# Second attention of a three-stage kernel: packed rows as the stationary operand, block-wise turns on VectorE, and two softmax steps on GpSimd

## The chip, the cores and the metric

One Trainium2 chip, one NeuronCore of it. The metric is the device time of one execution in microseconds (us). The kernel is one launch; its inputs and its output lie in the chip's memory (HBM). The engines are named as the profile names them: PE is TensorE (its matmuls) and PEld its weight loads, DVE is VectorE, ACT is ScalarE, POOL is GpSimd, and SP is SyncE, which starts most of the transfers.

## What is computed

Three layers follow each other: an attention in two steps, a mixture of eight experts of which every token takes two, and a feed-forward layer with SiLU. The change lies in the second step of the attention.

```python
def sm_attn(qq, kk, vv):
    s = scale * np.matmul(qq, kk.transpose(0, 1, 3, 2))      # scale = 1 / 8
    s = s - np.max(s, axis=-1, keepdims=True)
    a = np.exp(s)
    a = a / (np.sum(a, axis=-1, keepdims=True) + 1e-09)
    return np.matmul(a, vv)
p_packed = sm_attn(p, k, v)          # p [4, 8, 32, 64], k and v [4, 8, 576, 64]
out = sm_attn(q, p_packed, p_packed) # q [4, 8, 576, 64]: 32 keys for each of 576 tokens
...
x = out as [2304 tokens, 512]
logits = x @ w_gate; noise_scale = np.log1p(np.exp(x @ w_noise))
top2 of logits + noise_scale * noise; two experts relu(x @ w1[e]) @ w2[e], weighted
...
h = x @ w_in; out = (h / (1 + exp(-h))) @ w_out
```

## The kernel before

**Tiles and units.** The 2304 tokens are 18 tiles of 128. A tile is made of the tokens of one batch, or (two of the 18, `r == 8`) of the last 64 tokens of two batches. The first attention runs in eight units `packed(b, g)` of one batch and four heads, the second in ten units `unpacked(t, n, lg)`: eight of two tiles (`n` = 2) and two of one tile. Every unit is a generator with four steps, and the loop over `slot` (0 to 15) issues the steps of several units per slot, by the lists START1, START2, LAG1 and LAG2. After slot 9 the steps of `route(0, 11)`, the routing of the first 11 tiles, come in between; from slot 12 on (SWITCH) other PSUM pools are in use. The order on each engine is then set by the framework's planner, which works with its own costs; every engine runs its own queue strictly in order.

**`unpacked`, the function that is changed.** Step 1 turns q on PE (`qp`, L380) and copies it to `qT` (ACT). Step 2 makes the scores: a matmul with `qT` stationary (128 columns) and `ppT` moving (64 columns) per head, L387, or L394 for the one-tile units; the profile calls their output `s`. The scores lie in PSUM as tokens by (head, 32 keys). DVE takes the maximum (L397), subtracts it (L399), ACT takes the exponential (L400), DVE sums (L401), adds 1e-9 (L402), inverts (L403) and multiplies (L404). Step 3 turns the 128 x 128 pieces back on PE (`a2p`, L409) and copies them to `a2T` (ACT, L50 in the profile, the helper `cp`). Step 4 multiplies by `ppBD` (`xp`, L418, 272 columns: 256 of x and 16 logits), adds the two logit halves on DVE (L422, L420), copies x to `xr` (ACT) and writes `xr` to `xs` in HBM (SP, L425). `xr` has two buffers.

**What lies around it.** `packed` makes scores with 32 packed rows stationary at four column positions of the array and 256 columns of k moving (`s`, L320; 64 columns in L323), and in the same way `pp` (L346, 64 columns). POOL copies four pieces of `pp` to `ppBD` (L354) and makes the low halves of the first expert's weights (L111, 128 x 1024, eight times, `wa0l` to `wa7l`). The tiles `wa0h` to `wa7l` hold k and v first: `wa6l`, for one, is v of `packed(3, 0)`, so the split of `wa6l` must come after the `pp` matmuls of that unit. At the end `route(0, 11)` gives `idx0` (DVE, L502); POOL gathers rows with it (L154), PE turns them (`tps`, L144), and the first expert's matmuls (`hps`, L166 to L168; `acc`, L176 to L178) begin, with `route(11, 7)` beside them. What follows (experts 1 to 7 and the SiLU layer) is one dense run of matmuls.

Of the kernel before, what the change touches and what calls it, by code (L numbers as in the profile page):

```python
# [7 lines left out]
F32 = mybir.dt.float32  # L8
# [6 lines left out]
OP = mybir.AluOpType  # L15
AX = mybir.AxisListType
# [3 lines left out]
P = 128  # L20
# [4 lines left out]
CAP = ET * P  # L25
# [18 lines left out]
def body(ctx: ExitStack, tc: tile.TileContext, q, k, v, p, wg, wn, noise, w1, w2, w_in, w_out, out):  # L44
# [70 lines left out]
    def tick():  # L115
        """Finish the loads that were started DELAY ticks ago."""
        later.append(None)
        while later.count(None) > M["delay"]:
            fn = later.pop(0)
            if fn:  # L120
                fn()

    def load(dst, src, c, eng=V):
        """src [c * 128, 1024 / c] -> dst"""
# [14 lines left out]

    def transposed(src, xh, xl, j):  # L140
        """src [128 rows, 512] -> columns j*128.. of the split xh, xl [128, 4, n]"""
# [7 lines left out]
    def fetch(src, ix, c0, n):  # L149
        """The rows of src that the columns c0..c0+n-1 of ix name"""  # L150
# [8 lines left out]
    def first(ws, x, f, n):  # L159
        """[128 f, n] of w1.T x"""  # L160
# [55 lines left out]
    with ExitStack() as ax:  # L216
# [13 lines left out]
        # k, v and q wait in the tiles that the first expert and its rows will need  # L230
# [44 lines left out]
        # p turned, once above and once below zeros; group 0's second copy is the ninth  # L275
# [24 lines left out]
        def packed(b, g):  # L300
            """The packed rows of four heads, pp = softmax(p k^T / 8) v, in four steps."""
# [65 lines left out]
        def unpacked(t, n, lg):  # L367
            """x and the logits lg [128, n, 16] of tiles t..t+n-1, in four steps."""
# [14 lines left out]
            s2 = pS2[0].tile([P, n, 8, 32], F32, name="s2", tag="s2")  # L383
            if r < 8:
                b = parts[0][0]
                for h in range(8):
                    T.matmul(s2[:, :, h, :], qT[:, h, :], ppT[b, h // 4][:, h % 4], start=True, stop=True)  # L387
            else:
                for h in range(4):
                    for b, sl in parts:  # L390
                        o = 128 * (h % 2)
                        m = ppT[b, h // 2].rearrange("p j o k -> p (j o k)")
                        m = m[:, o:o + 128].rearrange("p (a k) -> p a k", a=4)[:, 0:4:3, :]
                        T.matmul(s2[sl, 0, 2 * h:2 * h + 2, :], qT[:, h, sl], m, start=True, stop=True)  # L394
            s2f = s2.rearrange("p n h k -> p (n h) k")
            mx = sb.tile([P, 3, 8 * n], F32, name=f"mx2{n}")
            V.tensor_reduce(mx[:, 0, :], s2f, axis=AX.X, op=OP.max)  # L397
            sd = sb.tile([P, 8 * n, 32], F32, name=f"sd{n}", tag="sd")
            V.tensor_tensor(sd, s2f, mx[:, 0, :, None].to_broadcast([P, 8 * n, 32]), op=OP.subtract)  # L399
# [4 lines left out]
            V.tensor_tensor(sd, sd, mx[:, 2, :, None].to_broadcast([P, 8 * n, 32]), op=OP.mult)  # L404
            yield
            anf = sd.rearrange("p a b -> p (a b)")
            ap = pTr.tile([P, 2 * n, P], F32, name="a2p", tag="tr")
            for i in range(2 * n):
                T.transpose(ap[:, i, :], anf[:, i * P:(i + 1) * P], ident)  # L409
            aT = sb.tile([P, 2 * n, P], F32, name=f"a2T{n}", tag="a2T", bufs=4)  # L410
            cp(A, aT, ap)
            yield
            for i in range(n):
                xr = sb.tile([P, 2, 256], F32, name="xr")
                for g in range(2):
                    xp = pMx.tile([P, 272], F32, name="xp", tag="m")
                    for b, sl in parts:
                        T.matmul(xp[sl], aT[:, 2 * i + g, sl], ppBD[b, g], start=True, stop=True)  # L418
                    if g:
                        V.tensor_tensor(lg[:, i, :], xp[:, 256:272], lg[:, i, :], op=OP.add)  # L420
                    else:
                        V.tensor_copy(lg[:, i, :], xp[:, 256:272])  # L422
                    cp(A, xr[:, g, :], xp[:, 0:256])
                r0 = (t + i) * P
                nc.sync.dma_start(xs[r0:r0 + P, :], xr.rearrange("p a b -> p (a b)"))  # L425
            yield

        def route(t0, n, lg):
            """Two experts, their gates and slots for the tiles t0..t0+n-1."""
# [3 lines left out]
            # log(1 + exp(z)) = log 2 + z / 2 + log(cosh(z / 2)); by its series where |z| <= 1/2  # L433
# [32 lines left out]
            # slot - 63.5 = CAP * expert + the number of earlier rows of the expert - 63.5  # L466
# [50 lines left out]
            # row of ys: the first TA tiles of all experts come before the others  # L517
# [48 lines left out]
        for slot in range(START2[-1] + LAG2[-1] + 1):  # L566
            if slot == SWITCH:
# [60 lines left out]
    def load64(raws, sbuf, src, last=None):  # L628
        """Loads src [128, a, b], float64 as words, 512 a row; the function returned makes its float32 value."""
# [15 lines left out]
    def routed():  # L645
        ctx = mx = ExitStack()
        with mx:
# [13 lines left out]
            def convert():  # L661
                """One [128, 512] piece of the float64 weights to its float32 values in DRAM"""
# [14 lines left out]
            def combine(m):  # L677
                t0, n = BLOCKS[m]
                xh, xl = X["ab"[m % 2]]
                # rows of the first TA tiles have earlier rows too few to fill more than TA tiles of an expert  # L680
# [220 lines left out]
```

## Time and profile before

| | |
|---|---|
| time, median of 3 runs | 1022.69 us (1022.52 to 1023.4) |
| the profiled execution, first to last instruction | 1020.1 us (its own device time is not given apart from this span) |
| PE busy | 987.6 us (97%), 6056 matmuls |
| DVE, ACT, POOL busy | 448.4 us (44%), 357.0 us (35%), 211.2 us (21%) |
| chain of work that ended last | PE 91%, DMA 3%, DVE 2%, ACT 1%, issue 1% |

The span is one execution under the profiler. A row of a group of instructions gives the line, engine and operation, output <- inputs, the form, the count, then the busy time and the mean of one, and last the idle time before them with what ended it. In the chain of waits each row is a start, a length and the work that ran; a chain follows back from the last instruction to whatever released each step. Matmuls overlap, so the pitch of a row of matmuls is read from the chain, where each piece counts once.

### The profile page before, as it was taken

To read this page: it belongs to the slowest core of one execution; us is meant where nothing else is said; L and a number is where in the kernel's file an instruction comes from. 1 tells how busy PE (TensorE), PEld (TensorE's weight loads), DVE (VectorE), ACT (ScalarE), POOL (GpSimd) and SP (SyncE) were. 2 spreads that over 40 slices of the span, in tenths; PEclk is the share of its full clock that TensorE was granted. 3 is DMA by queue.
4 is the path that set the end of the run, shared out by engine and by line. 5 is a ranking of instruction groups with operands and counts; after the bars stand their busy time and mean duration, and the time that the engine had idled before them with its cause. 6 is when DMAs were issued, how large, how long until landed. Compare 5 with 4: busy or idle time off the path is not lost.

```text
span 1020.1 us, 15287 instructions
## 1 busy us (share of the span) xinstructions
PE 987.6 (97%) x6056; PEld 876.7 (86%) x6056; DVE 448.4 (44%) x877; ACT 357.0 (35%) x693; POOL 211.2 (21%) x253
## 2 busy tenths in 40 slices
PE   6988798999999999999999998999999999999997
PEld 4766678899999989999998988999999999998996
DVE  3557762565656565665634447222232231112111
ACT  3566322443434343343423354222222222223332
POOL 2152011110101010010100117343232332222222
PEclk9998699999999999999999999999999999999999
DMA  9992224574756566574723445111110111000000
GB/s 247 246 274 88 73 73 157 189 234 148 228 179 221 186 206 204 184 236 152 234 86 101 137 154 166 52 31 32 36 39 19 52 31 31 1 1 32 1 21 21
DMA packets 80477, 122.53 MB, mean 120 GB/s; under 512 B 14608, under 2 KB 47376, under 8 KB 80400
## 3 DMA queue, kind: packets, MB, share of 16 engines
q1 hardware_dynamic: 74320, 101.57, 31.9%
q0 software_dynamic: 6080, 19.93, 6.5%
q8 instruction: 49, 0.80, 0.3%
q14 instruction: 28, 0.23, 0.1%
HBM read 93.17 MB, written 28.31 MB: 119 GB/s over the span
## 4 chain that ended last, share of the span: by engine, by line
PE 91%; DMA 3%; DVE 2%; ACT 1%; issue 1%; SPq 1%; POOL 0%; DVEq 0%; POOLq 0%; ACTq 0%
PE hps L166 14%; PE hps L168 14%; PE hps L167 14%; PE acc L177 13%; PE acc L178 13%; PE acc L176 13%; PE tps L144 2%; PE xp L418 2%; PE s L387 1%; PE s L320 1%; PE kp L309 1%; DMA raw<-in_moe_w_dram 1%; DMA km<-in_k_dram 1%; DMA ys<-ysb 1%; PE qp L380 1%
## 5 line engine op out<-in xcount | busy, mean ns | idle before, releaser
L697 DVE TENSOR_TENSOR sg<-hps,sg 128x384 f32<-128x384 f32 (+1 forms) x112 | 55.8, 499 | 242.4 <-ACT sg L696 242.4
L701 POOL TENSOR_TENSOR gl<-sg,gh 128x384 fp32r<-128x384 f32 (+1 forms) x112 | 102.1, 912 | 280.1 <-ACT gh L700 211.5
L189 ACT ACTIVATE hh<-hps 128x384 fp32r<-128x384 f32 (+1 forms) x128 | 56.1, 438 | 257.6 <-PE hps L168 247.1
L190 DVE SCALAR_TENSOR_TENSOR hl<-hps,hh 128x384 fp32r<-128x384 f32 (+1 forms) x128 | 62.6, 489 | 135.4 <-ACT hh L189 132.7
L696 ACT ACTIVATE sg<-hps 128x384 f32<-128x384 f32 (+1 forms) x112 | 49.9, 445 | 204.9 <-PE hps L168 204.6
L154 POOL DMA_INDIRECT xg<-xs,idx x40 | 40.8, 1019 | 354.7 <-PE tps L144 300.1
L700 ACT ACTIVATE gh<-sg 128x384 fp32r<-128x384 f32 (+1 forms) x112 | 53.6, 479 | 74.6 <-DVE sg L697 74.6
L687 POOL DMA_INDIRECT y<-ys,slots x36 | 36.4, 1012 | 98.7 <-DMA ys<-ysb 78.9
L147 DVE TENSOR_TENSOR xlb<-tps,xhb 128x512 fp32r<-128x512 f32 x32 | 22.0, 686 | 19.4 <-ACT xhb L146 19.2
L147 DVE TENSOR_TENSOR xla<-tps,xha 128x512 fp32r<-128x512 f32 x26 | 17.9, 690 | 27.8 <-ACT xha L146 25.8
L418 PE MATMUL xp<-ppBD,a2T 128*128 128x272 f32 (+1 forms) x80 | 26.5, 478 | 1.1 <-ACT xr L50 0.7
L146 ACT ACTIVATE xhb<-tps 128x512 fp32r<-128x512 f32 x32 | 19.1, 595 | 18.2 <-PE tps L144 17.3
L691 DVE SCALAR_TENSOR_TENSOR y<-y,gates,y 128x512 f32<-128x512 f32 x18 | 20.2, 1123 | 10.1 <-DMA y<-ys,slots 10.1
L144 PEld LDWEIGHTS tps<-ident,xg 128*128 128x128 f32 x160 | 19.9, 142 | 5.4 <-issue 0.5
L144 PE MATMUL tps<-ident,xg 128*128 128x128 f32 x160 | 23.9, 273 | 0.2 <-issue 0.2
L146 ACT ACTIVATE xha<-tps 128x512 fp32r<-128x512 f32 x26 | 15.5, 597 | 21.2 <-PE tps L144 21.1
L640 DVE SCALAR_TENSOR_TENSOR t<-raw,t 128x512 int32<-128x512 int32 x32 | 22.2, 693 | 1.1
L641 DVE SCALAR_TENSOR_TENSOR t<-raw,t 128x512 int32<-128x512 int32 x32 | 22.1, 692 | 1.1
L166 PE MATMUL hps<-xha,wa3h 128*128 128x256 f32 (+1 forms) x64 | 19.6, 306 | 2.7 <-DVE sg L697 2.7
L166 PE MATMUL hps<-xhb,wa0h 128*128 128x384 f32 (+1 forms) x56 | 19.2, 343 | 3.0 <-issue 3.0
L690 DVE TENSOR_SCALAR y<-y,gates 128x512 f32<-128x512 f32 x18 | 10.1, 559 | 26.5 <-DMA y<-ys,slots 26.5
L52 DVE COPY ysb<-acc 128x512 f32<-128x512 f32 x24 | 16.5, 686 | 11.2 <-PE acc L178 11.2
(438 smaller groups left out, 3112.4 us busy)
## 6 DMA issues: line engine op xcount, KB each, us to landing
raw<-in_moe_w_dram SPq DMA_DIRECT2D x64, 512.0 KB
ys<-ysb SPq DMA_DIRECT2D x40, 256.0 KB
raw<-in_moe_w_in_dram SPq DMA_DIRECT2D x16, 512.0 KB
raw<-in_moe_w_out_dram SPq DMA_DIRECT2D x16, 512.0 KB
xs<-xr SPq DMA_DIRECT2D x18, 256.0 KB
km<-in_k_dram SPq DMA_DIRECT2D x8, 512.0 KB
vm<-in_v_dram SPq DMA_DIRECT2D x8, 512.0 KB
qm<-in_q_dram SPq DMA_DIRECT2D x8, 512.0 KB
```

Of the source, the lines that this page charges most:

```text
L144: pin(T.transpose(ps[:, c, :], src[:, c * P:(c + 1) * P], ident))
L166: T.matmul(ps, wh[:, c, s], xh[:, c, :n], start=c == 0, stop=False)
L167: T.matmul(ps, wh[:, c, s], xl[:, c, :n], start=False, stop=False)
L168: T.matmul(ps, wl[:, c, s], xh[:, c, :n], start=False, stop=c == 3)
L176: T.matmul(y, hh[:, s], wh[:, f % 2, :], start=f == 0, stop=False)
L177: T.matmul(y, hh[:, s], wl[:, f % 2, :], start=False, stop=False)
L178: T.matmul(y, hl[:, s], wh[:, f % 2, :], start=False, stop=f == last)
L189: A.activation(hh, ps, AF.Relu)
L190: V.scalar_tensor_tensor(hl, ps, 0.0, hh.bitcast(F32), op0=OP.max, op1=OP.subtract)
L697: V.tensor_tensor(sg, ps, sg, op=OP.mult)
L700: A.activation(gh, sg, AF.Copy)
L701: G.tensor_tensor(gl, sg, gh.bitcast(F32), op=OP.subtract)
```

## The change

`unpacked` is changed from its second step on. The scores are made with 32 packed rows of `ppT` stationary at column position 32 j and 128 columns of `qT` moving (64 in the one-tile units), so that they lie as (head, key) by token. DVE turns them in blocks of 32 x 32 from PSUM into `sd`, with one instruction of 512 columns (256 in the one-tile units); after it every group of 32 columns is the row of one token and head. The maximum, the sum, the addition of 1e-9 and the reciprocal stay on DVE; the subtraction of the maximum and the multiplication by the reciprocal are moved to POOL. A second block-wise turn on DVE gives `aT` directly; the PE transposes `a2p` and their ACT copy are gone, and `aT` has three buffers where it had four. ACT copies all 272 columns of `xp` to `xr`, POOL adds the two logit halves out of `xr`, and the write of `xs` takes 256 of every 272 columns of `xr`. The rest of the diff takes comments away.

```diff
-            s2 = pS2[0].tile([P, n, 8, 32], F32, name="s2", tag="s2")
+            s2 = pS2[0].tile([P, 2, n * P], F32, name="s2", tag="s2")
             if r < 8:
                 b = parts[0][0]
-                for h in range(8):
-                    T.matmul(s2[:, :, h, :], qT[:, h, :], ppT[b, h // 4][:, h % 4], start=True, stop=True)
+                for g in range(2):
+                    for o in range(2):
+                        for j in range(4):
+                            T.matmul(s2[32 * j:32 * j + 32, g, o * P:(o + 1) * P], ppT[b, g][:, j, o, :], qT[:, 4 * g + j, :],
+                                     start=True, stop=True, tile_position=(0, 32 * j))
             else:
-                for h in range(4):
+                for g in range(2):
                     for b, sl in parts:
-                        o = 128 * (h % 2)
-                        m = ppT[b, h // 2].rearrange("p j o k -> p (j o k)")
-                        m = m[:, o:o + 128].rearrange("p (a k) -> p a k", a=4)[:, 0:4:3, :]
-                        T.matmul(s2[sl, 0, 2 * h:2 * h + 2, :], qT[:, h, sl], m, start=True, stop=True)
-            s2f = s2.rearrange("p n h k -> p (n h) k")
+                        for j in range(4):
+                            T.matmul(s2[32 * j:32 * j + 32, g, sl], ppT[b, g][:, j, j % 2, :], qT[:, 2 * g + j // 2, sl],
+                                     start=True, stop=True, tile_position=(0, 32 * j))
+
+            sd = sb.tile([P, 8 * n, 32], F32, name=f"sd{n}", tag="sd")
+            sdf = sd.rearrange("p a b -> p (a b)")
+            V.transpose(sdf, s2.rearrange("p g c -> p (g c)"))
             mx = sb.tile([P, 3, 8 * n], F32, name=f"mx2{n}")
-            V.tensor_reduce(mx[:, 0, :], s2f, axis=AX.X, op=OP.max)
-            sd = sb.tile([P, 8 * n, 32], F32, name=f"sd{n}", tag="sd")
-            V.tensor_tensor(sd, s2f, mx[:, 0, :, None].to_broadcast([P, 8 * n, 32]), op=OP.subtract)
+            V.tensor_reduce(mx[:, 0, :], sd, axis=AX.X, op=OP.max)
+            G.tensor_tensor(sd, sd, mx[:, 0, :, None].to_broadcast([P, 8 * n, 32]), op=OP.subtract)
             A.activation(sd, sd, AF.Exp, scale=0.125)
             ...
-            V.tensor_tensor(sd, sd, mx[:, 2, :, None].to_broadcast([P, 8 * n, 32]), op=OP.mult)
-            yield
-            anf = sd.rearrange("p a b -> p (a b)")
-            ap = pTr.tile([P, 2 * n, P], F32, name="a2p", tag="tr")
-            for i in range(2 * n):
-                T.transpose(ap[:, i, :], anf[:, i * P:(i + 1) * P], ident)
-            aT = sb.tile([P, 2 * n, P], F32, name=f"a2T{n}", tag="a2T", bufs=4)
-            cp(A, aT, ap)
+            yield
+            G.tensor_tensor(sd, sd, mx[:, 2, :, None].to_broadcast([P, 8 * n, 32]), op=OP.mult)
+            aT = sb.tile([P, 2, n * P], F32, name=f"a2T{n}", tag="a2T", bufs=3)
+            V.transpose(aT.rearrange("p g c -> p (g c)"), sdf)
             yield
             for i in range(n):
-                xr = sb.tile([P, 2, 256], F32, name="xr")
+                xr = sb.tile([P, 2, 272], F32, name="xr")
                 for g in range(2):
                     xp = pMx.tile([P, 272], F32, name="xp", tag="m")
                     for b, sl in parts:
-                        T.matmul(xp[sl], aT[:, 2 * i + g, sl], ppBD[b, g], start=True, stop=True)
-                    if g:
-                        V.tensor_tensor(lg[:, i, :], xp[:, 256:272], lg[:, i, :], op=OP.add)
-                    else:
-                        V.tensor_copy(lg[:, i, :], xp[:, 256:272])
-                    cp(A, xr[:, g, :], xp[:, 0:256])
+                        T.matmul(xp[sl], aT[:, g, i * P + sl.start:i * P + sl.stop], ppBD[b, g], start=True, stop=True)
+                    cp(A, xr[:, g, :], xp)
+                G.tensor_tensor(lg[:, i, :], xr[:, 0, 256:272], xr[:, 1, 256:272], op=OP.add)
                 r0 = (t + i) * P
-                nc.sync.dma_start(xs[r0:r0 + P, :], xr.rearrange("p a b -> p (a b)"))
+                nc.sync.dma_start(xs[r0:r0 + P, :].rearrange("p (g c) -> p g c", g=2), xr[:, :, 0:256])
             yield
```

## Rows read from the trace of the kernel before

**Rows 1.** Busy time per stage, all engines.

```profile
core 0: us, PE busy (x) PEld busy (x) DVE busy (x) ACT busy (x) POOL busy (x), PEclk, DMA share, GB/s
...
25.00:62.00 37.00, 33.73 (x503) 26.46 (x502) 20.47 (x53) 21.63 (x51) 7.75 (x18) 1.00 0.98 259
...
62.00:95.00 33.00, 29.00 (x271) 21.87 (x271) 21.91 (x63) 24.64 (x59) 13.64 (x10) 0.94 0.53 182
...
95.00:122.00 27.00, 22.45 (x170) 18.07 (x171) 20.97 (x97) 7.83 (x21) 6.22 (x11) 0.57 0.15 48
...
158.00:1020.00 862.00, 854.09 (x4764) 774.13 (x4764) 355.74 (x553) 284.50 (x522) 172.45 (x181) 1.00 0.35 112
```

**Rows 2.** Chain of waits, 25 to 62 us: start, length, work (x pieces).

```profile
36.67 0.84 PE s L387 x8
...
43.16 0.65 PE pp L346 x32
...
44.83 0.59 PE qp L380 x4
...
45.42 1.00 PE s L320 x16
...
48.46 0.44 PE a2p L409 x4
...
52.62 8.54 DMA raw<-in_moe_w_dram
```

**Rows 3.** Chain of waits, 62 to 160 us.

```profile
63.42 0.88 PE s L394 x16
...
71.39 2.03 issue
...
97.25 1.90 PE s L387 x8
...
111.44 3.21 DVE rt_oa L492 x4
```

**Rows 4.** Busy time per stage of line L387 alone (PE and PEld).

```profile
25.00:62.00 37.00, 8.30 (x64) 7.76 (x64) 1.00 0.98 259
...
95.00:122.00 27.00, 6.68 (x32) 6.50 (x32) 0.57 0.15 48
```

**Rows 5.** The same of line L409 alone.

```profile
62.00:95.00 33.00, 2.85 (x18) 2.13 (x18) 0.94 0.53 182
...
95.00:122.00 27.00, 2.81 (x10) 1.98 (x10) 0.57 0.15 48
```

**Rows 6.** Busy time in two shorter stretches, columns as in Rows 1.

```profile
44.00:50.00 6.00, 6.00 (x86) 4.92 (x85) 2.35 (x8) 4.42 (x13) 0.92 (x4) 1.00 0.30 65
...
95.00:108.00 13.00, 12.50 (x102) 10.18 (x103) 9.43 (x66) 4.20 (x13) 4.15 (x9) 0.50 0.07 25
```

**Rows 7.** Groups of instructions by form (DVE, ACT 0 to 140 us).

```profile
L399 DVE TENSOR_TENSOR sd<-s,mx 128x512 f32<-128x512 f32 x8 | 5.5, 684 | 1.2 <-PE a2p L409 1.0
...
L50 ACT ACTIVATE a2T<-a2p 128x512 f32<-128x512 f32 x8 | 4.9, 610 | 7.9 <-PE a2p L409 7.9
...
L701 POOL TENSOR_TENSOR gl<-sg,gh 128x384 fp32r<-128x384 f32 x64 | 66.0, 1031 | 182.9 <-ACT gh L700 175.4 <-DMA y<-ys,slots 7.5
...
L701 POOL TENSOR_TENSOR gl<-sg,gh 128x256 fp32r<-128x256 f32 x48 | 36.1, 754 | 97.2 <-PE acc L178 60.7 <-ACT gh L700 36.1 <-issue 0.2
...
L354 POOL COPY ppBD<-px 32x64 f32<-32x64 f32 x32 | 7.8, 243 | 40.7 <-DVE px L349 24.3 <-DVE mx L331 7.8 <-DVE mx L327 7.6
```

**Rows 8.** Instructions in order of time; in brackets the idle time before.

```profile
71.25 2.25 DVE L404 TENSOR_TENSOR sd<-sd,mx 128x256 f32<-128x256 f32 x1
...
92.39 2.35 POOL L111 TENSOR_TENSOR wa6l<-raw,wa6h 128x1024 fp32r<-128x1024 f32 x1 [15.01 <-ACT rt_sa L439]
...
92.45 2.39 DVE L447 TENSOR_TENSOR rt_sa<-rt_sa,lg 128x88 f32<-128x88 f32 x1
...
95.16 0.47 PE L356 MATMUL tp<-ident,px 128*128 128x128 f32 x1 [2.51 <-DVE px L349]
```

## The prediction

> **What bounds the kernel now.** I read the busy time by stage first. From 158 us to the end PE is busy 854 of 862 us [rows 1]; the change has nothing there, so the end moves by as much as that dense run starts earlier. Everything that is changed runs between 25 and 122 us, in three stages: 25 to 62 us, with PE busy 33.7 of 37 us and the DMA engines at 0.98; 62 to 95 us, PE 29.0 of 33 and DMA 0.53; 95 to 122 us, PE 22.5 of 27, but at a granted clock of 0.57, with DVE busy 21.0 of the 27 [rows 1]. The reader is to see a PE that is nearly full, first beside full transfers, then alone, then at half speed beside a nearly full DVE. Second I read the chain of waits. In the first stage it runs through PE and then through one weight transfer of 8.5 us [rows 2]; afterwards through PE, with pieces of DVE's softmax and routing at the end [rows 3]. Third, the instructions around 92 us show how the slow stretch begins: POOL starts a weight split (L111, 2.35 us), DVE starts a routing step of 88 columns 0.06 us later, and that step takes 2.39 us and ends just after POOL; `px` behind it and PE's `tp` come late, PE idles 2.51 us [rows 8], and the 13 us after it run at a granted clock of 0.50, the lower of the two levels, 1.2 GHz [rows 6].
>
> **Part 1, the scores on PE.** One unit of two tiles has 16 records of L387, two chain pieces of eight at 0.84 us: 1.68 us [rows 2]. The new form has 16 float32 matmuls, so 32 records, each with 32 stationary columns and 128 moving. No row has that shape. Its neighbours have the same four column positions: `pp` with 64 moving columns, 32 records in 0.65 us (20 ns each), and L320 with 256, 16 in 1.00 us (62 ns each) [rows 2]. On the line between them 128 columns cost 34 ns, 32 records 1.10 us; the bounds are 0.65 and 2.00 us. I take 1.10: a unit saves 0.58 us (from 1.03 saved to 0.32 lost). Of the 128 records 64 lie before 62 us and 32 after 95 us, so 32 between [rows 4]: four, two and two units. In the last stage 32 records are busy 6.68 us against 8.30 / 2 = 4.15 in the first, 1.6 times as much (a piece of eight took 1.90 us at 97 us [rows 3]), and so are savings there. That makes 2.3 us before 62, 1.2 us between, 1.9 us after 95. The two one-tile units go from 0.88 us [rows 3] to the shape of `pp`, 0.65: 0.23, and 0.37 in the slow stage, together 0.6.
>
> The chain shows `qp` end at 45.42 us and L320 begin at 45.42 us, so going from the full array to column positions leaves no gap [rows 2]. The Trainium skill (TensorEngine Tiling (Array Packing), Key Properties) says that a change of tiling mode drains TensorE, which speaks against twenty more of such changes; by that rule the time is the one of the third rival below, and this trace does not agree with it.
>
> **Part 2, the transposes on PE.** All 36 `a2p` go. Four are a piece of 0.44 us [rows 2], 0.11 us each. 18 lie between 62 and 95 us and 10 after [rows 5], so 8 before. Busy time of one is 0.158 us in the middle stage and 0.281 in the last, 1.8 times. That makes 0.9, 2.0 and 2.0 us.
>
> **Part 3, what of this arrives.** After 62 us PE saves 1.2 + 1.9 + 0.6 + 2.0 + 2.0 = 7.7 us, and there these pieces are the chain. Before 62 us it saves 3.2 us beside transfers that run at 0.98, and the chain passes to a transfer at 52.6 us [rows 2]; yet between 44 and 50 us the DMA share is only 0.30 [rows 6], since SP's loads wait for buffers that PE must leave first. An earlier PE fills part of that hole. Bounds 0 and 3.2; I take half, 1.6 us.
>
> **Part 4, logits.** The DVE copies and additions out of `xp` go, and with them a place where ACT's copy of `xp` waits for DVE. On the chain this is a piece of 2.03 us: the logits' addition came at 73.4 us, since it stood behind a multiplication L404 that took 2.25 us [rows 3, 8]. I take 1.5 us (0 to 2.4). The 16 columns more per `xp` copy on ACT are covered, since ACT is busy 54.1 us of the 97 [rows 1]. The write of `xs` stays 18 issues on SP, in pieces half as long; the DMA engines have room for it after 62 us, at 0.53 and 0.15 [rows 1], so I cost it at nothing; if a write took 1 us more, `xr` with its two buffers would be late by that once at the end.
>
> **Part 5, what is added.** POOL's subtraction and multiplication of 512 columns: two-input POOL rows take 0.754 us for 256 columns and 1.031 for 384 [rows 7], 2.16 ns a column, so 1.31 us for 512. DVE took 0.684 [rows 7]. 16 such, 4 of 0.75 and 18 small additions (nearest row 0.243, rows 7) are 28.4 us more on POOL, which is busy 27.6 of the 97 us [rows 1]: 58%, so it isn't full. The block-wise turn has no row; as the nearest, a 512-column pass of DVE is 0.684 us. I take that; the bounds are 0.61, ACT's pass of 512 [rows 7], and twice the value, 1.37. DVE then does four passes of 512 where it did four, so its load hardly changes. The Trainium skill (VectorE: DVE Perf Modes, The three transpose paths) gives 311 ns for a 128 x 128 block turn in bf16, an estimate of 1.24 us for four of them; no row here shows one, and by it the sum would be some 2 us higher (0.56 us for each of four turns in the last two units).
>
> Latency of one unit, without the steps that stay: before, maximum, subtraction, multiplication (0.68 each), `a2p` 0.44 and `a2T` 0.61 [rows 2, 7], 3.1 us; after, turn 0.68, maximum 0.68, 1.31 + 1.31 on POOL, turn 0.68, 4.7 us. So +1.6 us a unit. In the middle the distance of two slots between step 2 and step 4 covers it, with PE at other units. At the end, with three units left and DVE nearly full, it does not: 2.5 us (0 to 4.8).
>
> New waits: DVE's sum and second turn now stand behind POOL, and DVE's queue behind them. Also, as shown at 92 us, a DVE step with two inputs in SBUF waits out a POOL instruction. The softmax of the last units runs beside the routing, whose step L492 alone is 3.21 us [rows 3]. I count three hits of half a POOL instruction, 2.0 us (0 to 7, five hits of a full one). The logits take the way over ACT and POOL before the routing starts, twice 0.25: 0.5 us.
>
> **Sum.** Gains 7.7 + 1.6 + 1.5 = 10.8, costs 2.5 + 2.0 + 0.5 = 5.0: 5.8 us less. The profiled execution would go from 1020.1 to 1014.3 us; the median of the runs is 2.6 us above that span and keeps this distance: 1016.9, say 1017 us.
>
> **Rivals.** First, *slower*: POOL's order. The split of `wa6l` stood ready, but POOL idled 15.01 us before it [rows 8], because its buffer holds v of the last batch until `pp` has read it. POOL is in order: a subtraction or multiplication planned behind that split (or behind `wa7l`'s) waits for `pp`, and then DVE's turn and PE's `xp` wait too. Each such stop that PE can't fill costs what the one at 92 us does, 2.5 us, and a slow stretch of which I count a quarter of 13 us, 3.3 [rows 6, 8]. One stop cancels the gain; two, 11.6 us, give 1022.7 - 5.8 + 11.6 = 1028.5. For it: POOL goes from 28% to 58%. Against: the splits' place in the plan is late, after most units.
>
> Second, *no change*: the savings are on PE only, and the start of the dense run hangs on the routing, which is DVE's: then only the logits' 1.5 us and part of the slow stage's saving stay, against the 5.0 us of costs, 1022 us. For it: DVE busy 21.0 of 27 us [rows 1]. Against: PE fills the chain in 62 to 95.
>
> Third, drains: twenty units' changes into and out of column positions, each at 0.2 us (half of the 0.47 us that one matmul took at the lower clock, rows 8), cost 4 us: 1021 us. Against it: no gap at 45.42.
>
> Fourth, *more gain*: POOL's and DVE's instructions fall differently and the stop at 92.4 us, with the slow clock after it, does not come. PE's 12.5 us busy at 0.50 [rows 6] would need 6.3; 6 us more: 1011 us. That the change doesn't do what it says is possible only if the column positions do not run side by side; L320's 62 ns for 256 columns exclude it.
>
> **Chances.** Forecast 0.42, slower 0.25, no change 0.10, drains 0.05, more gain 0.18. The measurement can tell about 0.2%, 2 us. Faster by more: 0.42 + 0.18 and 0.01 of the drains, 0.61; within: 0.10 and the rest of the drains, 0.14; slower: 0.25. The range reaches from 1008 (more gain with the scores at their better bound) to 1029 (two stops).
>
> **What would show it.** Right: a group of 32 records of the new scores near 1.1 us in the chain; no `a2p`; POOL near 55 us busy in 25 to 122, its 512-column steps near 1.3 us; the dense run starting near 152 us. Wrong: PE idle for over 2 us before `xp` with DVE's turn or POOL as releaser; a POOL multiplication behind `wa6l`; a slow clock in 62 to 95; turns over 1 us. The forecast fails first if the last two units' softmax, not PE, sets `idx0`.

## The result, and the profile after

| | median, us | lowest to highest | span of the profiled execution |
|---|---|---|---|
| before | 1021.8 | 1017.1 to 1023.9 | 1020.1 |
| after | 1026.3 | 1023.8 to 1031.5 | 1029.0 |

The changed kernel takes 1.0060 of the time before, 95% interval [1.0043, 1.0078]: 6 us longer (the medians alone lie 4.5 us apart), where 6 us shorter was forecast. 1026.3 lies in the range of 1008 to 1029, on the side of the rivals. The profiled execution of after (1030.8 us) is the second slowest of its twelve, which has to be kept in mind for every row below.

The stages of after, as in [rows 1] (us; busy time and count of each engine; granted clock, DMA share, GB/s):

```profile
core 0: us, PE busy (x) PEld busy (x) DVE busy (x) ACT busy (x) POOL busy (x), PEclk, DMA share, GB/s
25.00:62.00 37.00, 32.80 (x588) 23.16 (x580) 19.21 (x48) 19.31 (x50) 13.47 (x29) 0.96 0.99 255
62.00:95.00 33.00, 28.55 (x273) 17.87 (x271) 15.93 (x39) 24.21 (x53) 21.80 (x23) 0.84 0.59 189
95.00:122.00 27.00, 16.44 (x200) 9.68 (x200) 23.13 (x90) 5.26 (x16) 12.07 (x18) 0.59 0.11 36
...
161.00:1029.00 868.00, 856.14 (x4764) 774.61 (x4764) 354.24 (x553) 284.51 (x522) 175.71 (x181) 0.99 0.35 111
```

PE is less busy in each of the three stages than in [rows 1] (16.44 us against 22.45 in the last), and nothing ends earlier. DVE in the last stage has risen from 20.97 to 23.13 us. The dense run has the same 4764 instructions as in [rows 1], but lasts 868 us in place of 862.

The new instructions by form, 0 to 140 us (busy us in total, mean ns of one):

```profile
L404 POOL TENSOR_TENSOR sd<-sd,mx 128x512 f32<-128x512 f32 x8 | 8.4, 1050 | 16.5 <-DVE mx L403 10.1 <-DVE mx L407 6.2
...
L401 DVE STREAM_TRANSPOSE sd<-s 128x512 f32<-128x512 f32 x8 | 5.7, 709 | 3.4 <-PE s L390 3.4
L412 DVE STREAM_TRANSPOSE a2T<-sd 128x512 f32<-128x512 f32 x8 | 5.6, 703 | 3.5 <-POOL sd L410 3.4
```

Four matmuls run side by side, so the length of one record of the new scores (L390, 313 ns) says little. In the chain 32 of them are 1.01 us, close to the 1.10 taken. A turn of 512 columns is 0.70 to 0.71 us (0.684 taken), a POOL step of 512 columns 1.05 us (1.31 taken). Prices were not the fault.

The tail of after in order of time, the last full units beside the routing (idle time before, and what ended it, in brackets):

```profile
105.46 0.71 DVE L401 STREAM_TRANSPOSE sd<-s 128x512 f32<-128x512 f32 x1
...
106.97 1.07 POOL L404 TENSOR_TENSOR sd<-sd,mx 128x512 f32<-128x512 f32 x1 [1.97 <-DVE mx L403]
...
112.63 3.29 DVE L490 TENSOR_TENSOR rt_oa<-iota_lo,rt_lo 128x768 f16<-128x768 f16 x4
...
116.59 1.05 POOL L404 TENSOR_TENSOR sd<-sd,mx 128x512 f32<-128x512 f32 x1 [6.23 <-DVE mx L407]
...
117.60 1.05 POOL L410 TENSOR_TENSOR sd<-sd,mx 128x512 f32<-128x512 f32 x1
...
118.81 1.15 POOL L154 DMA_INDIRECT xg<-xs,idx  x1 [0.17 <-issue]
...
119.69 0.82 PE L419 MATMUL xp<-ppBD,a2T 128*128 128x272 f32 x1 [3.40 <-DVE a2T L412]
```

One unit needs 14 us from its turn at 105.46 to its `xp` at 119.69. DVE is passed three times (turn and maximum, sum and reciprocal, second turn), and each pass queues behind routing steps; the fetch of the first expert's rows stands behind POOL's multiplication. PE idles 3.40 us for it. A wait of over 2 us before `xp` with DVE's turn as releaser was the prediction's first sign of being wrong. I read it as POOL's handovers, and that was my first theory (it is near the first rival, but that one asks for a stop behind a weight split). The second thing in this trace I did not expect at all. The chain of waits where the dense run begins, after:

```profile
159.09 2.15 issue
161.23 0.52 PE hps L166
...
162.72 0.32 PE hps L167
163.04 2.73 issue
165.77 0.48 PE hps L168
...
171.69 0.20 PE hps L168
```

and the same place before:

```profile
155.65 2.42 issue
158.06 0.41 PE hps L166
```

"Issue" is time in which PE waited for nothing that the profile shows. Both kernels have 2.2 to 2.4 us of it at the branch into the dense part; after has 2.73 us more, five matmuls later.

### The profile page after: what moved, and what is told of

Read it like the earlier page. It is cut to its first block, busy times and chain, and to the rows that moved or that the text cites. A ratio compares the mean times of both kernels' runs of the same rounds, so it can differ in the third digit from the quotient of the medians.

```text
span 1029.0 us, 15501 instructions
## 1 busy us (share of the span) xinstructions
PE 984.3 (96%) x6180; PEld 862.8 (84%) x6180; DVE 442.9 (43%) x841; ACT 353.0 (34%) x683; POOL 236.7 (23%) x291
## 4 chain that ended last, share of the span: by engine, by line
PE 87%; DMA 4%; DVE 3%; ACT 2%; issue 1%; POOL 1%; SPq 0%; ACTq 0%; DVEq 0%; POOLq 0%
PE hps L166 14%; PE hps L168 14%; PE hps L167 14%; PE acc L177 13%; PE acc L176 13%; PE acc L178 13%; PE tps L144 2%; DMA km<-in_k_dram 1%; DMA raw<-in_moe_w_dram 1%; PE xp L419 1%; PE s L320 1%; PE s L390 1%; PE kp L309 1%; DVE rt_oa L490 1%; PE qp L380 0%
## 5 line engine op out<-in xcount | busy, mean ns | idle before, releaser
L699 POOL TENSOR_TENSOR gl<-sg,gh 128x384 fp32r<-128x384 f32 (+1 forms) x112 | 104.2, 931 | 279.9 <-ACT gh L698 211.6
L419 PEld LDWEIGHTS xp<-ppBD,a2T 128*128 128x128 f32 (+1 forms) x80 | 12.9, 208 | 11.7 <-ACT xr L50 4.7
L168 PE MATMUL hps<-xhb,wa0l 128*128 128x384 f32 (+1 forms) x56 | 19.7, 352 | 2.7 <-issue 2.7
```

The costliest lines, as they stand in the source:

```text
L168: T.matmul(ps, wl[:, c, s], xh[:, c, :n], start=False, stop=c == 3)
L699: G.tensor_tensor(gl, sg, gh.bitcast(F32), op=OP.subtract)
```

## The experiments

Theories: **A**, the handovers to POOL lengthen the tail. **B**, PE's savings do not arrive. **C**, the logits' way over ACT and POOL is late. Later came **D**, loading of PE's code, and **E**, DVE's load in the tail. All ratios are to the kernel before, measured beside each; their intervals are within 0.0015 to 0.003 either way.

| kernel | median, us | ratio | dense run begins | from there to the end | second stop |
|---|---|---|---|---|---|
| before | 1021.8 | 1 | 158.06 | 862.0 | none |
| after | 1026.3 | 1.0060 | 161.23 | 867.8 | 2.73, after 5 matmuls |
| e1_dve | 1030.0 | 1.0084 | 162.25 | 866.0 | 1.34, after 7 |
| e2_tail | 1030.5 | 1.0084 | 163.77 | 865.4 | 2.66, after 4 |
| e3_logits | 1028.6 | 1.0066 | 163.07 | 865.5 | none, but 7.17 at the branch |
| e4_lg_dve | 1027.6 | 1.0062 | 157.36 | 865.7 | 3.19, after 6 |
| p_after | 1022.1 | 0.9992 | 158.75 | 861.7 | none |
| q_after | 1023.3 | 1.0023 | 156.59 | 861.6 | none |
| p_before | 1025.2 | 1.0026 | 160.07 | 868.2 | 2.92, after 5 |
| q_before | 1027.3 | 1.0046 | 158.51 | 867.2 | 3.78, after 1 |
| p_e1 | 1025.4 | 1.0029 | 160.51 | 861.9 | none |
| p_e3 | 1021.1 | 0.9996 | 158.46 | 861.5 | none |
| p_e4 | 1024.0 | 1.0023 | 159.88 | 862.9 | none |
| p_e5 | 1030.3 | 1.0083 | 168.25 | 861.9 | none |
| w_after | 1017.8 | 0.9962 | 155.75 | 861.7 | none |
| w_before | 1018.2 | 0.9975 | 155.27 | 861.6 | none |

The columns on the dense run are from one profiled execution each: its first matmul in the order of time, and the span less that. That execution is not always a typical one: p_before's (1030.1 us) is the slowest of its twelve, q_after's (1020.0 us) the second fastest of its twelve.

### Parts undone, and one alone

**e1_dve** puts the softmax's two POOL steps back on DVE:

```diff
-            G.tensor_tensor(sd, sd, mx[:, 0, :, None].to_broadcast([P, 8 * n, 32]), op=OP.subtract)
+            V.tensor_tensor(sd, sd, mx[:, 0, :, None].to_broadcast([P, 8 * n, 32]), op=OP.subtract)
...
-            G.tensor_tensor(sd, sd, mx[:, 2, :, None].to_broadcast([P, 8 * n, 32]), op=OP.mult)
+            V.tensor_tensor(sd, sd, mx[:, 2, :, None].to_broadcast([P, 8 * n, 32]), op=OP.mult)
```

> The changed kernel with the subtraction of the maximum and the multiplication by the reciprocal on DVE (both edits of the softmax's engine undone for all ten units; scores, turns and logits stay changed). Theory A, the handovers to POOL lengthen the tail: in the changed kernel unit 7 goes from its scores' turn at 105.5 us to its xp at 119.7 us, because DVE is passed three times and each time queues behind routing steps; without POOL the last logits come near 128 us again (132.5 in the changed kernel, 128.2 before) and the dense run starts near 157 us: 1020 to 1022 us, 4 to 6 less than the changed kernel's 1026.3. Theory B, the savings on PE never arrive and the longer chain is due to the turns and the logits' way: 1025 to 1028. Theory C, what the logits cost: 1025 to 1027, unchanged here.

**e2_tail** does so for the last units alone:

```diff
-            G.tensor_tensor(sd, sd, mx[:, 0, :, None]...
+            (V if t >= EARLY else G).tensor_tensor(sd, sd, mx[:, 0, :, None]...
...
-            G.tensor_tensor(sd, sd, mx[:, 2, :, None]...
+            (V if t >= EARLY else G).tensor_tensor(sd, sd, mx[:, 2, :, None]...
```

> The changed kernel with the subtraction and multiplication on DVE only for the units from tile 11 on, and on POOL for the earlier ones. Theory A: as without POOL at all or better, since only the last units stand beside the routing: 1019 to 1022 us, dense run starting near 157 us. If instead POOL's stop at 92 us and the later transfers of the first stages are what costs: 1024 to 1027, as the changed kernel. Theories B and C: 1025 to 1028.

**e3_logits** is the kernel before with the logits' part alone:

```diff
-                    if g:
-                        V.tensor_tensor(lg[:, i, :], xp[:, 256:272], lg[:, i, :], op=OP.add)
-                    else:
-                        V.tensor_copy(lg[:, i, :], xp[:, 256:272])
-                    cp(A, xr[:, g, :], xp[:, 0:256])
+                    cp(A, xr[:, g, :], xp)
+                G.tensor_tensor(lg[:, i, :], xr[:, 0, 256:272], xr[:, 1, 256:272], op=OP.add)
```

> The kernel before with the logits' change alone (xp copied by ACT with 272 columns, both halves added by POOL, the write of xs from 256 of 272 columns, three buffers of the turned softmax). Theory C, the way over ACT and POOL makes the logits late: 2 to 4 us above the kernel before, 1024 to 1026. Theory A: within 1 us of the kernel before, since the tail's order is set by DVE's softmax: 1021 to 1023. My prediction put it at 1.0 below: 1.5 gained, 0.5 lost.

**e4_lg_dve** is the changed kernel with this part undone (the diff above, turned round).

> The changed kernel with the logits taken out of xp by DVE as before (that part undone; scores, turns and POOL's two steps stay). Theory C: 2 to 4 us below the changed kernel, 1022 to 1024. Theory A: no better than the changed kernel, 1026 to 1028, since DVE in the tail gets 36 small steps back. Theory B: 1025 to 1027.

Measured: 1.0084, 1.0084, 1.0066 and 1.0062. No theory has this pattern. A falls: it forecast 4 to 6 us less without POOL's steps, and the kernel is not faster but 2 to 4 us slower. And the logits alone cost as much as the whole change, while the change without them costs the same. So the whole change, three variants of it and one part of it alone all lose 0.6 to 0.8% against a single kernel, the one before. The table's last two columns show why: in all of them the time from the first dense matmul to the end is 865.4 us or more against 862.0, though that part is the same code. In e3_logits the chain shows PE standing at the branch for 7.17 us:

```profile
155.91 7.17 issue
163.07 0.69 PE hps L166
```

### Code loading: the same instructions at another place

The DMA queues show what comes at these moments. In after, from 162.5 to 163.0 us, and from 158.0 to 158.5 us (packets, MB, share of the 16 engines):

```profile
q1 hardware_dynamic: 125, 0.13, 90.8%
q8 instruction: 1, 0.02, 19.9%
...
q8 instruction: 1, 0.02, 14.4%
```

Queue q8 carries one packet of code at a time; the page of after counts 51 with 0.84 MB, some 16 KB each. I take that as 256 instructions of 64 bytes, which the counts below will test. Its packets stand at 158.4 and 162.8 us in after; PE starts 2.8 us after the first and again 3.0 us after the second. In before they stand at 155.4 and 159.9 us, with a start 2.7 us after the first and no stop at the second. So I read it like this: PE's code comes in pieces, this branch waits for the piece with its target, and the next piece comes some 4.5 us later, beside the transfers that fill the queues there (90.8% above). PE stops if it has run the first piece to its end by then.

How far that is hangs on where the target lies in its piece, and so on how many PE instructions stand ahead of it. Counting them in the programs (a matmul of float32 is two records, each with a load of its stationary side, hence 4; a transpose 2; and PE's separate waits), after has 243 more ahead of the branch's target than before, and e3_logits 2 fewer. If before's target is the first instruction of a piece, 256 are left in the piece there, 13 in after, 16 in e1_dve, 11 in e2_tail, 14 in e4_lg_dve, 2 in e3_logits. If two instructions stand ahead of the first matmul and each record takes two, that makes 5, 7, 4, 6 and 0 matmuls up to the end of the piece, which are the numbers in the table. One offset, assumed and shown by no trace, fits five kernels. How long PE stops hangs on the second packet as well: in e1_dve it comes 3.1 us after the first, and the stop is only 1.34 us.

The next four test it. They leave each executed instruction as it is and put transposes, which never run, into the general case, whose code lies ahead of the dense part:

```diff
                 for c in range(4):
                     T.transpose(ps[:, c, :], src[:, c * P:(c + 1) * P], ident)
+                for _ in range(8):
+                    T.transpose(ps[:, 3, :], src[:, 3 * P:4 * P], ident)
```

**p_after** is the changed kernel with it.

> The changed kernel, every executed instruction the same; the part of the program that is not taken (the general case, which lies ahead of the dense part in PE's code) has 16 transposes more, so the dense part begins some 32 PE instructions further on. Theory D, code loading: in the trace PE's code comes in pieces of 16 KB (queue q8, 256 instructions of 64 bytes); at the branch into the dense part PE waits 2.7 to 2.9 us for the piece with the target, and in the changed kernel this piece ends after 5 matmuls, so that PE stops 2.7 us again and then runs at half clock to 172 us; in the kernel before the piece lasted until the next one was there. By the counts of PE's instructions the target stands 13 instructions before the end of a piece in the changed kernel and at the start of one in the kernel before; with the shift it is 237 before the end. The second stop goes, with part of the half clock: 4 to 5 us, 1021 to 1023. Rival, the stop comes from the weight loads that start at the same time, wherever the code stands: unchanged, 1025 to 1028.

**p_before** is the kernel before, with 61 in place of 8.

> The kernel before, every executed instruction the same, with 122 transposes (244 PE instructions) more in the part that is not taken: by the counts the dense part's first piece of code then ends after 12 instructions, as in the changed kernel. Theory D: a second stop of 2.5 to 3.5 us after about 4 matmuls of the dense part and half clock after it: 3 to 5 us above the kernel before, 1024 to 1026. Rival, the loads: unchanged, 1020 to 1022.

**p_e1** is e1_dve with 8.

> The changed kernel with both softmax steps on DVE and the same 32 PE instructions of shift as in the shifted changed kernel. Against the latter it shows what POOL's two steps cost or give without the stop in the code. Theory D: 3 to 5 us below the unshifted one (1030.0): 1025 to 1027, and so still above the shifted changed kernel: POOL's handovers are then not the cost. If handovers cost (theory A): below the shifted changed kernel, 1018 to 1020. Rival, the loads: 1029 to 1031.

**p_e3** is e3_logits with 8.

> The kernel before with the logits' change alone, shifted by 32 PE instructions (by the counts its target stood 2 instructions before the end of a piece, so that PE waited for two pieces, 7.2 us, before its first matmul). Theory D: the stop becomes 2.9 us, 4 to 6 us less than the 1028.55 unshifted: 1022 to 1024; what is left above the kernel before is the price of the logits' way, 1 to 3 us. Rival, the loads: 1027 to 1029.

In all four the stop went or came as D says; the sizes came less well. The changed kernel loses the second stop and goes from 1.0060 to 0.9992 [0.9976, 1.0008]; e1_dve goes from 1.0084 to 1.0029, the logits alone from 1.0066 to 0.9996, 1 us below the range that D had for it. The kernel before, at 1025.2 us, lies in its range, but against the unshifted one that is 0.26%, 2.7 us, where 3 to 5 were expected. Their chain at the branch, p_after:

```profile
156.67 2.08 issue
158.75 0.41 PE hps L166
```

and the kernel before gets the stop, after the fifth matmul, as the rule above gives for the 12 instructions left (the expectation had said about four):

```profile
160.07 0.66 PE hps L166
...
162.01 2.92 issue
164.93 0.69 PE hps L168
```

The stop itself is nearly half of the price in these traces; the clock is most of the rest. From 160 to 170 and 170 to 180 us, after (columns as above):

```profile
160.00:170.00 10.00, 6.03 (x19) 5.87 (x20) 0.56 (x1) 0.49 (x1) 4.72 (x5) 0.57 0.94 331
170.00:180.00 10.00, 10.00 (x49) 9.26 (x48) 1.47 (x3) 1.48 (x3) 0.00 (x0) 0.92 0.12 43
```

and p_after:

```profile
160.00:170.00 10.00, 10.00 (x47) 9.43 (x46) 1.67 (x3) 1.48 (x3) 4.72 (x5) 0.83 0.90 324
170.00:180.00 10.00, 10.00 (x53) 9.25 (x53) 2.46 (x4) 2.57 (x5) 0.00 (x0) 1.00 0.07 24
```

In after the granted clock is at its lower level, 1.2 GHz, from the first matmul on (161.4 us), thus before the second stop already, until about 171.7 us; without that stop, in p_after, only from 159.9 to 163.3 us. Of the 6.1 us between the two dense runs (867.8 less 861.7) 2.7 are the stop; 2.4 are PE busy for longer with the same 4764 instructions (856.14 us against 853.76 in p_after), which is the clock; 1 us is idle time in other places.

Two more ask for the size, since p_before lost only 0.26%. **q_before** has 63 transposes in before, **q_after** 36 in after.

> The kernel before, every executed instruction the same, shifted by 252 PE instructions (126 transposes in the part that is not taken): by the counts the first piece of code ends 4 instructions after the target, ahead of the first matmul. Theory D: PE waits for two pieces at the branch, 6 to 8 us in place of 3 (as in the kernel with the logits alone, 7.2 us), 1.004 to 1.008 of the kernel before. If a place of the code costs only what the shift by 244 did: 1.002 to 1.004.

> The changed kernel, every executed instruction the same, shifted by 144 PE instructions: by the counts the first piece ends 125 instructions after the target, some 60 matmuls and some 10 us of work. Theory D: no second stop, as with the shift by 32 (0.9992 of the kernel before): 0.998 to 1.001. If the gain of that shift was chance and hangs on one place: 1.003 to 1.007.

The expectation had put q_before's stop ahead of the first matmul, with 6 to 8 us at the branch. It comes after one matmul, as the rule above gives for 4 instructions left, two of them ahead of the matmul:

```profile
158.51 0.41 PE hps L166
158.92 3.78 issue
162.70 0.69 PE hps L167
```

It takes 1.0046 [1.0029, 1.0063]. q_after shows no second stop in its trace and a dense run of 861.6 us, but its executions scatter from 1019.9 to 1028.4 us and its ratio is 1.0023 [1.0005, 1.0040], between the two expectations; whether its slow executions have a second stop isn't shown.

So the place costs the kernel before 2.6 to 4.7 us and the other kernels 4 to 7; in the traces the dense run is 865.4 to 868.2 us with a stop or a long wait and 861.5 to 862.9 without, 4.7 us apart on average. Why some medians show less is open (a second packet that comes earlier, as in e1_dve, would shorten the stop), and so is what separates q_after from p_after.

The next packet of q8 bears the counts out where PE does not stop. By the counts 127 matmuls are left in the first piece in before, 117 in p_after, 112 in p_e3 and 61 in q_after. The third packet comes after 109 matmuls of the dense run in before (at 180.6 us), after 97 in p_after (178.9), 90 in p_e3 (177.2) and 44 in q_after (166.2): 17 to 22 matmuls ahead of the counted end each time, wherever that end lies.

### The parts, with the code's place the same

**p_e4** is e4_lg_dve with the 8 transposes. **p_e5** has the new scores and the turns alone: both edits of e1_dve and that of e4_lg_dve, with the 8.

> The changed kernel with the logits taken out by DVE as before, with the same 32 PE instructions of shift as in the shifted changed kernel (1022.05 us, 0.9992 of the kernel before). It shows what the logits' part is worth beside the other parts. My prediction: that part gains 1.0 (1.5 less 0.5), so without it about 1 us above the shifted changed kernel. Theory C, the way over ACT and POOL brings the last logits and the writes late: 2 to 3 us below it (the unshifted one reached the branch at 154.9 us in its trace, against 156.7 in the shifted changed kernel). Theory E, DVE is the tail's bound and the 36 small steps come back to it: 2 to 4 us above it.

> The new scores and the two turns alone: subtraction and multiplication on DVE, logits on DVE as before, shifted by 32 PE instructions. Theory E, DVE is the tail's bound: two turns a unit (0.70 us each) come in on DVE and nothing leaves it, so 3 to 6 us above the kernel before, and above the one with both softmax steps on DVE and the new logits (1.0029 of before). Theory of my prediction, PE's saving of 7.7 us after 62 us arrives: 3 to 6 us below the kernel before.

| | logits on DVE | logits over ACT and POOL |
|---|---|---|
| both softmax steps on DVE | 1.0083 (p_e5) | 1.0029 (p_e1) |
| both on POOL | 1.0023 (p_e4) | 0.9992 (p_after) |

The new scores and turns by themselves cost 0.83%, 8.5 us. Moving the two steps to POOL gives 6.1 us back, moving the logits 5.5, both 9.3; each of these differences is uncertain by 2.5 to 3.5 us. Each move takes work off DVE, and each gives time: that is what theory E says, though no run loads DVE and nothing else. The traces bear it out in the waits for `rt_oa`, the routing's longest step on DVE, ahead of the first expert's rows. Its start scatters too much to be read (112.63, 108.91 and 106.11 us in after, p_after and q_after, which run the same instructions), but PE's wait for it is 3.5 us in each of these three. Us in total, times, longest, in p_e5:

```profile
PE ip L500 <- DVE rt_oa L493: 8.8, 5, 7.1
```

in p_e1:

```profile
PE ip L497 <- DVE rt_oa L490: 9.4, 5, 7.8
```

and in the kernel before:

```profile
PE ip L499 <- DVE rt_oa L492: 1.7, 4, 0.5
```

In p_e4 it is 7.6 us. The wait does not follow the time in every step (p_e1 is 5.5 us faster than p_e5), so it is not the whole of it. Of the expectations, E's for p_e4 is met (3.2 us above p_after, where C said 2 to 3 below); p_e5 is 8.5 us above the kernel before, more than E's 3 to 6.

### The stop at 92 us

**w_after** and **w_before** take the two weight splits that hold DVE there off POOL; both also have the 8 transposes:

```diff
-                        load_w2(W[0], 0, i - 4, G)
+                        load_w2(W[0], 0, i - 4, G if i < 6 else V)
```

> The shifted changed kernel with the splits of wa6l and wa7l on DVE in place of POOL, so that no POOL instruction of 2.35 us holds DVE's routing steps at 92 us. Rival 4 of my prediction priced that stop and the half clock after it at 6 us; the idle time alone is 2.5 us. If that price is right: 1016 to 1019. If DVE bounds what follows (two splits of 1.22 us come to it): 1021 to 1025, no gain or a loss.

> The kernel before with the splits of wa6l and wa7l on DVE, shifted by 32 PE instructions (224 instructions before the end of a piece, so the shift by itself costs nothing). If the stop at 92 us is worth 2.5 to 6 us: 0.994 to 0.9975 of the kernel before. If DVE bounds what follows: 1.000 to 1.003.

0.9962 [0.9943, 0.9980] and 0.9975 [0.9954, 0.9997]. In before the step held there was L447 [rows 8]; in after it is another one, L438:

```profile
94.27 2.13 DVE L438 TENSOR_SCALAR rt_h<-rt_w 128x88 f32<-128x88 f32 x1
```

In w_after it is back at its own length; the split runs on DVE behind it, for 1.22 us:

```profile
94.35 0.20 DVE L438 TENSOR_SCALAR rt_h<-rt_w 128x88 f32<-128x88 f32 x1
```

The whole edit is worth about 3 us in either kernel (0.9992 to 0.9962, and 0.25% of before; the kernel before with the 8 transposes and nothing else was not run). w_after, at 1017.8 us, is the fastest of all, 4 us below the kernel before. The two w kernels lie 0.4 us apart and their intervals overlap, so beside this edit no gain of the change itself is shown.

## Why the prediction was wrong, point by point

**The premise.** "From 158 us to the end PE is busy 854 of 862 us; the change has nothing there, so the end moves by as much as that dense run starts earlier." Its instructions are the same, but their place in PE's code is not, and that made 862.0 into 867.8 us. No term of the sum and no rival had it. This is the step that turned little or no change into slower: with the code's place changed and nothing else, 1.0060 becomes 0.9992 (p_after) or 1.0023 (q_after). The Trainium skill (Runtime: NRT & Kernel Launch, Instruction fetch mechanics) says that code is fetched in pieces of 16 KB and that a taken branch stalls for the piece of its target when that piece isn't there yet; the traces agree (2.1 to 2.8 us at the branch). It also calls the cost of crossing into the next piece mostly hidden; right behind the branch it is not, with 1.3 to 3.8 us. A hint of it was in the trace of before: the 2.42 us of issue at the branch.

**Part 3, what arrives on PE.** 7.7 us after 62 us and 1.6 before were the gains. The stages of p_after, which has no second stop:

```profile
25.00:62.00 37.00, 32.73 (x589) 23.30 (x586) 19.08 (x47) 21.29 (x53) 14.89 (x30) 0.99 0.99 260
62.00:95.00 33.00, 26.28 (x283) 16.81 (x285) 18.25 (x45) 22.20 (x51) 22.29 (x26) 0.91 0.52 177
95.00:122.00 27.00, 17.75 (x198) 11.31 (x187) 22.89 (x89) 7.12 (x19) 11.79 (x18) 0.56 0.15 49
```

From 62 to 122 us PE is busy 44.0 us against 51.5 in [rows 1], 7.4 less: the saving on PE was sized right. In a stretch of fixed length it is idle 7.4 us more by that alone (16.0 against 8.6). That the saving did not arrive shows in the medians, 0.9992 (p_after) and 1.0023 (q_after) of the kernel before, where 0.994 was forecast. The longest waits of PE in p_after, 25 to 157 us (us in total, times, longest):

```profile
PE xp L419 <- ACT xr L50: 3.7, 3, 2.0
PE ip L497 <- DVE rt_oa L490: 3.5, 5, 1.9
PE xp L419 <- DVE a2T L412: 3.4, 1, 3.4
PE tp L356 <- DVE px L349: 2.5, 1, 2.5
```

and in before:

```profile
PE a2p L409 <- DVE sd L404: 2.6, 1, 2.6
PE tp L356 <- DVE px L349: 2.5, 1, 2.5
...
PE xp L418 <- ACT xr L50: 0.7, 2, 0.5
```

So what grew is the wait for ACT's copies of `xp` (0.7 to 3.7 us) and that for `rt_oa` (1.7 to 3.5), while the long one for DVE's softmax went from 2.6 to 3.4. The chain shows it more plainly than the waits. Of the chain between 90 and 114 us, PE has 14.4 us and DVE 5.8 in before; in p_after DVE has 20.9 and PE 1.4 (14.1 and 7.3 in after, 17.2 and 4.9 in q_after). In p_after:

```profile
68.31 1.01 PE s L390 x32
...
95.98 2.07 DVE rt_sp L446
...
108.99 3.21 DVE rt_oa L490 x4
...
115.09 3.53 DMA xg<-xs,idx
```

where before has PE's scores and `xp` up to 109 us:

```profile
106.40 2.56 PE s L387 x16
```

The second rival said this, with a chance of 0.10: the start of the dense run hangs on DVE's routing. Its time, 1022, is that of p_after. "PE fills the chain in 62 to 95" was the argument against it, and the failing one: a chain through a busy engine says where time went, not what is late next once that engine gets faster. In the first stage PE is busy 1.0 us less. The weight transfer that ends that stage's chain is over at 61.16 us before ([rows 2], 52.62 and 8.54), and at 61.76, 59.38 and 58.75 in after, p_after and q_after, so whether any of the 1.6 us that I took arrived there can't be told.

**Parts 1 and 2, the prices.** Right: 1.01 us for 32 of the new scores (1.10 taken), no `a2p`, 0.70 us for a turn (0.684 taken). The Trainium skill (VectorE: DVE Perf Modes, The three transpose paths) gave an estimate of 1.24 us for a turn from its bf16 figure, and a sum 2 us higher; the measured 0.709 us goes against that estimate.

**Part 4, logits.** Sized at 1.0 us of gain; alone it is 0.4 us with an uncertainty of 1.5 (p_e3), beside the other parts 3.2 (p_after against p_e4) to 5.5 (p_e1 against p_e5). The reason given, a place where ACT waits for DVE, can't be the main one, since it is there in p_e3 too; the table points to DVE's relief.

**Part 5, what is added.** The sign was wrong. POOL's two steps were counted as cost (2.5 us of latency and 2.0 of held DVE steps); they give 3.8 us (p_after against p_e1) to 6.1 (p_e4 against p_e5), and DVE, which the turns had filled, is the likely reason. "DVE then does four passes of 512 where it did four, so its load hardly changes" is true only of the whole change: without POOL it is six. The latency is there, 14 us for one unit in after; how much of it other work hides isn't measured. POOL is busy 47.3 us in 25 to 122 (13.47, 21.80 and 12.07), not 56, as its steps are shorter and some fall behind 122 us. DVE steps are held in after (2.13 us for L438, 1.93 for L446), as L447 was before [rows 8].

**Rival 1, a stop behind POOL's order.** Nearest in size (slower, up to 1028.5), and chance had it so: but its mechanism is in none of these traces. The row it rests on names ACT's `rt_sa`, not `pp`, as what ended POOL's 15.01 us [rows 8]. In after the split of `wa6l` waits 0.23 us for `pp`, and the softmax steps that wait on POOL do so for DVE (1.97 us at 106.97, 6.23 at 116.59).

**Rival 3, drains.** In p_after's chain the pieces before and after column positions touch (`xp` at 46.05 for 0.92 us, then the new scores at 46.97), as before the change. **Rival 4, more gain.** The stop at 92 us did not vanish in after: L438 is held in place of L447, and PE's `tp` comes as late (2.5 us for `px` in both). Taking it away is worth about 3 us, not 6.

## What to carry to other kernels

Where a program branches into its long part, every edit ahead of the branch moves the long part's code, and a loss or gain of half a per cent may be that alone: compare the time from the first instruction behind the branch to the end, and shift the code without changing what runs before judging an edit. When an engine that fills the chain is relieved, add up the next engine's queue over the same stretch first; 7 us less of work on PE moved nothing here, since DVE, busy 21 of 27 us, took PE's place in the chain. And a step that costs an engine time is best judged by which engine it leaves, not by its own length: POOL's 1.05 us in place of 0.68 on DVE made the kernel 4 to 6 us faster.

## What the runs showed of the hardware that I had not expected

- PE's code arrives in packets of some 16 KB (51 for 0.84 MB). At this branch the first matmul starts 2.5 to 3.1 us after the packet is seen, and the next packet follows 3.1 to 4.7 us after the first (all sixteen kernels; in e3_logits the matmul starts after the second). By the counts, a target 4 to 16 instructions ahead of a piece's end cost 1.3 to 3.8 us of standing PE, and one 2 instructions ahead 7.2 us at the branch.
- Behind the wait at the branch the granted clock falls to its lower level, 1.2 GHz, in p_after and after. It comes back after 3.4 us in p_after (159.9 to 163.3 us), which does not stop again, and after 10 us in after (161.4 to 171.6), which does.
- A DVE step with one SBUF source (L438, 128x88) and a predicated copy (L446, 128x88) are held by a POOL subtraction of 1024 columns, too: 2.13 and 1.93 us in after, 0.20 and 0.26 us in w_after.
- The same executed instructions reach the dense run at times up to 4.6 us apart from execution to execution (161.23, 158.75 and 156.59 us in after, p_after and q_after), while the dense run without the stop repeats to 0.5 us in eight kernels of nine.
